# Gated mix of two memory attentions on one core: order of the short scores, the entry of P times v, the last output block, and a new table of rules

## The chip, the core and the metric

The kernel runs on one core of a Trainium2 chip. The time is device microseconds of one execution, the median of several runs. TensorE (PE) multiplies matrices out of SBUF into PSUM banks, VectorE (DVE), ScalarE (ACT) and GpSimd (POOL) do the elementwise work, and SyncE (SP) issues the DMAs.

## The reference

The input x has 2048 tokens of 640 features. Two attentions, A and B, with 32 heads of 20 features, are computed on it and mixed with a gate for each token. Each attention goes through four segments of 512 tokens. In a segment a query sees the keys of its own segment up to itself (a causal softmax), and a memory that sums up all earlier segments:

```python
logits = jnp.einsum("bhqd,bhkd->bhqk", qs, ks) * scale + mask
p = _softmax(logits, axis=-1)
a_dot = jnp.einsum("bhqk,bhkd->bhqd", p, vs)
num = jnp.einsum("bhld,bhde->bhle", phi(qs), M)      # M, z: sums over earlier segments
den = jnp.einsum("bhld,bhd->bhl", phi(qs), z)[..., None] + 1e-6
o = g * num / den + (1.0 - g) * a_dot                # g: one number for each head
M = M + jnp.einsum("bhld,bhle->bhde", phi(ks), vs)
z = z + jnp.einsum("bhld->bhd", phi(ks))
```

`phi(t)` is t + 1 above zero and exp(t) below. The o of all heads is multiplied by wo (640 x 640), and the result is gate * A + (1 - gate) * B.

## The kernel before

The work is cut into eight parts t = 0 to 7 (segment t // 2, attention t % 2), and each part's scores into eight *quads* of four heads, 64 quads in all. Every matrix of a product is split into two parts (high and low) that are multiplied in three combinations, (high, high), (low, high), (high, low).

**Two lanes.** Most matmuls use 64 or fewer of the 128 rows of TensorE's array. The kernel gives the lower half and the upper half of the rows a stream of matmuls each, the two *lanes*, and the two run side by side. P times v (`pv_unit`, L1396) uses all 128 rows, so it begins only when both lanes have ended, and the lanes begin again behind it. The update of the memory (L1029) may follow it directly.

**Units.** For each quad there are five S units (`s_unit`, L1283: query rows times keys, from which VectorE takes each query's maximum, L1268), five T units (`t_unit`, L1375: the scores again, transposed and with the maximum in two extra rows; ScalarE takes the exponential, L1367, and GpSimd cuts the triangle, L1368; the result is P) and one P times v. The causal triangle makes scores of 128, 256, 384 and 512 columns. `S_UNITS` and `T_UNITS` say which scores share a PSUM bank, and in which order their matmuls run: an entry (pair, block, offset) has 128 x (block + 1) columns in S units and 512 - 128 x block columns in T units. So of the S units the second and fourth have a 128 and a 384, and of the T units the third and fourth a 384 and a 128.

Between the units stand the *products* (`product`, recorded at L818): q, k and v of the next part, and the outputs. There are also transposes (`turn`, L971), in groups of four for each lane, and the reading of the memory (`mem_unit`, L929).

**The planner.** The order of the instructions is not written out. At build time a planner goes along with a modelled clock: `lane` holds when each lane ends, `lane_step` picks what a lane does next, and modelled events (DMAs landing, engines ending) set what can be picked. Where a lane has just ended on a matmul that is shorter than the loading of weights, `quick` is set for it, and `lane_step` then takes a waiting transpose first if there is one.

A table, `RULES`, has one line for each quad step i. Its fields: the order of the five S (of quad i + 2) and five T units (of quad i), and then `span`, `calm`, `lag`, `room`, `hold`, `wait`, `wait2` and `pair`. `wait` is how long a transpose waits for a quick lane before it is started as other work is. With `pair` 1 the P times v of quad i - 1 is held until the one after it can run too, and the two go back to back; a hold is not set where the P times v before it is held already.

`step` is the planner's loop. When a P times v is due and its P is there, it asks `aligned`: P times v goes if the two lanes end within 0.07 us of each other in the model, or after eight tries; each try that fails lets a lane take one more step.

**The end.** The last part's output is begun early for the first three of five row blocks of wo (`job_early`) and finished by `job_last` (L1210), with all 128 rows: for each of the five blocks of 128 output features three matmuls of 512 columns per remaining row block, and then `finish`: VectorE adds what was kept (L1195), and SyncE stores the block (L1197).

Of the kernel before, what the change touches and what calls it, by code (L numbers as in the profile page):

```python
# [18 lines left out]
P = 128  # L19
D = 640  # L20
# [22 lines left out]
def tile_gated_mix_infini_attn(  # L43
# [1142 lines left out]
    def job_last(t):  # L1186

        s = t // 2
        pps = {}

        def finish(m):
            if m not in kept:
                at(clk[0] + 0.3, lambda: finish(m))
                return
# [678 lines left out]
```

## Time and profile before

| | |
|---|---|
| median of 3 runs | 980.11 us (977.87 to 980.46) |
| profiled execution, its own time | 980.22 us |
| its span, first to last instruction | 978.4 us |
| TensorE busy | 968.8 us, 99% |
| VectorE, ScalarE, GpSimd busy | 75%, 69%, 64% |
| TensorE's granted clock, mean | 0.999 |
| DMA moved | 236.47 MB, 242 GB/s |

How to read it: an engine's busy time is the union of its instructions' spans, and a matmul's span covers its wait inside the array, so a TensorE that is 99% busy can still lose time between two matmuls. A group's row has its line, engine, operation, what it writes and reads, the shape, the count, and behind the first bar the busy time and the mean duration of one in ns; behind the second bar is the idle time before it. A row in order of time has its start, the time from its first start to its last end, and what ran; matmuls of both lanes stand in one list. A row of the waits has who waited, on whom, the sum in us, the count and the longest.

### The profile page before, as it was taken

The page shows a single profiled execution, that of the slowest core. Times are in us where ns is not written, and L with a number is a line of the kernel's source. Part 1 is how long each engine was busy: PE and PEld are TensorE (multiplying, and loading weights), DVE is VectorE, ACT ScalarE, POOL GpSimd, SP SyncE. Part 2 cuts the span into 40 slices and gives each one's busy share as a digit, 9 for nine tenths or more (in the row PEclk, how much of TensorE's full clock was granted, in tenths as well). Part 3 has the DMA queues.
Part 4 walks back from the last instruction along what each step waited for, and adds up shares of the span by engine and source line. Part 5 has one row for each costly group of instructions (what it writes and reads, how often), then busy time and mean ns, then how long its engine had stood idle before and what let it go on. Part 6 is the DMA issues. An engine that isn't in the chain of part 4 may idle for free.

```text
span 978.4 us, 31660 instructions
## 1 busy us (share of the span) xinstructions
PE 968.8 (99%) x11559; PEld 830.3 (85%) x11559; DVE 736.8 (75%) x2635; ACT 671.8 (69%) x1425; POOL 628.5 (64%) x1168
## 2 busy tenths in 40 slices
PE   9999999999999999999999999999999999999998
PEld 7998888888898888899878888798888888889785
DVE  4686777975787686886689986588676996788863
ACT  5476777777767587767676676676677666785672
POOL 4366657876568565768566577477765666666671
PEclk9999999999999999999999999999999999999999
DMA  6999988898888887977689777699777879877531
GB/s 214 309 312 260 298 259 286 252 301 269 257 282 243 268 269 218 305 216 228 190 244 294 225 222 208 206 296 289 216 231 235 271 223 264 242 227 240 155 92 54
DMA packets 146454, 236.47 MB, mean 242 GB/s; under 512 B 12950, under 2 KB 45883, under 8 KB 145979
## 3 DMA queue, kind: packets, MB, share of 16 engines
q1 hardware_dynamic: 146298, 234.46, 78.6%
q8 instruction: 91, 1.49, 0.7%
q14 instruction: 65, 0.52, 0.2%
HBM read 145.26 MB, written 94.65 MB: 245 GB/s over the span
## 4 chain that ended last, share of the span: by engine, by line
PE 91%; DMA 4%; DVE 1%; POOL 1%; issue 1%; ACT 1%; SPq 0%; ACTq 0%; POOLq 0%
PE bank L818 54%; PE bank L1396 14%; PE bank L1283 9%; PE bank L1375 7%; PE bank L929 3%; PE bank L971 3%; DMA wst<-in_a_wk_dram 1%; PE bank L1029 1%; DMA qst<-qd 1%; DMA kd<-row 1%; DMA kst<-kd 1%; PE bank L1210 0%; DVE row L1195 0%; POOL row L1502 0%; POOL row L1509 0%
## 5 line engine op out<-in xcount | busy, mean ns | idle before, releaser
L818 PE MATMUL bank<-row,wh 64*128 64x512 f32 x2308 | 484.9, 399 | 0.2
L818 PEld LDWEIGHTS bank<-row,wh 64*128 64x128 f32 x2308 | 319.8, 185 | 13.9 <-issue 1.6
L1268 DVE CUSTOM_DVE_ANT_0 junk<-bank,tri 128x128 bf16<-128x128 f32 (+2 forms) x768 | 278.9, 419 | 64.5 <-PE bank L1283 47.0
L1367 ACT ACTIVATE p<-bank 128x512 f32<-128x512 f32 x470 | 255.1, 601 | 89.7 <-PE bank L1375 75.5
L818 PE MATMUL bank<-row,wl 64*128 64x512 f32 x1154 | 297.4, 395 | 0.0
L1368 POOL TENSOR_SCALAR_AFFINE_SELECT p<-p 128x256 f32<-128x256 f32 (+1 forms) x470 | 171.9, 379 | 122.7 <-ACT p L1367 113.7
L555 POOL TENSOR_TENSOR wl<-wst,wh 128x640 fp32r<-128x640 f32 x115 | 179.8, 1569 | 68.6 <-ACT wh L557 62.8
L1268 DVE CUSTOM_DVE_ANT_0 bank<-bank,tri 128x512 f32<-128x512 f32 x256 | 172.5, 711 | 42.8 <-PE bank L1283 38.1
L1283 PE MATMUL bank<-kst,qst 60*128 60x128 f32 (+3 forms) x1024 | 179.5, 328 | 2.3 <-ACT p L1367 1.7
L818 PEld LDWEIGHTS bank<-row,wl 64*128 64x128 f32 x1154 | 176.7, 186 | 5.5 <-issue 0.6
L1375 PE MATMUL bank<-qst,kst 62*128 62x384 f32 (+3 forms) x1024 | 171.2, 316 | 0.0
L818 PE MATMUL bank<-wvh,row 64*128 64x320 f32 (+1 forms) x1280 | 169.7, 311 | 0.0
L818 PEld LDWEIGHTS bank<-wvh,row 64*128 64x128 f32 x1280 | 145.2, 186 | 2.2 <-issue 1.0
L1283 PEld LDWEIGHTS bank<-kst,qst 60*128 60x128 f32 x1024 | 129.6, 185 | 11.7 <-ACT p L1367 2.1
L1375 PEld LDWEIGHTS bank<-qst,kst 62*128 62x128 f32 x1024 | 129.0, 186 | 7.6 <-issue 1.0
L1396 PE MATMUL bank<-p,vst 128*32 128x128 f32 (+3 forms) x1536 | 117.5, 429 | 0.3 <-DVE mx L1268 0.3
L557 ACT CAST wh<-wst 128x640 fp32r<-128x640 f32 x119 | 86.9, 738 | 40.7 <-PE bank L818 18.1
L1367 ACT ACTIVATE row<-bank 128x512 f32<-128x512 f32 x170 | 92.8, 599 | 25.7 <-PE bank L1375 24.6
L1396 PEld LDWEIGHTS bank<-p,vst 128*32 128x32 f32 x1536 | 47.0, 110 | 67.5 <-issue 50.7
L1268 DVE DVE_READ_ACCUMULATOR2_ANT mx<- 128x1 f32 x1024 | 100.2, 98 | 0.0
L818 PE MATMUL bank<-wvl,row 64*128 64x320 f32 (+1 forms) x640 | 98.2, 310 | 0.0
L1368 POOL TENSOR_SCALAR_AFFINE_SELECT row<-row 128x128 f32<-128x128 f32 (+1 forms) x170 | 58.6, 352 | 54.9 <-ACT row L1367 50.4
(122 smaller groups left out, 1261.0 us busy)
## 6 DMA issues: line engine op xcount, KB each, us to landing
qst<-qd SPq DMA_DIRECT2D x128, 240.0 KB
kst<-kd SPq DMA_DIRECT2D x128, 240.0 KB
qd<-row SPq DMA_DIRECT2D x40, 512.0 KB
kd<-row SPq DMA_DIRECT2D x40, 512.0 KB
dots<-row SPq DMA_DIRECT2D x56, 256.0 KB
wst<-wmix SPq DMA_DIRECT2D x35, 320.0 KB
row<-dots SPq DMA_DIRECT2D x42, 256.0 KB
qd<-row SPq DMA_DIRECT2D x40, 256.0 KB
```

The source lines that it names most:

```text
L555: put(lo_eng, lo_cost, lambda: lo.tensor_tensor(out=wl, in0=w3, in1=r32(wh), op=ALU.subtract), end, prio=3)
L557: put("A", 0.625, lambda: nc.scalar.copy(wh, w3), low, prio=6)
L818: return nc.tensor.matmul(bank_of, lhsT=w[ROWS[half]], rhs=x_[ROWS[half]], start=start, stop=stop)
L929: return nc.tensor.matmul(pm[:, a - h0:c - h0, :].rearrange("p h e -> p (h e)"), lhsT=r32(pqTs[t, m][ROWS[half], P * n:P * (n + 1)]), rhs= ...
L971: return nc.tensor.transpose(px[:, n, r], block(n)[r], ident[r, r])
L1029: nc.tensor.matmul(v[r, a - LO[m]:c - LO[m], :].rearrange("p h e -> p (h e)"), lhsT=r32(pkn[:, P * n + r.start:P * n + r.stop]), rhs=vst[t ...
L1268: nc.vector.tensor_tensor_reduce(out=sc[:, off:off + w] if w == L else junk[:, at_:at_ + w], in0=sc[:, off:off + w], in1=tri[:, L - w:], s ...
L1283: lane_ops[half].append((mm(w), lambda pair=pair, qb=qb, off=off, w=w, r=r, sc=sc: nc.tensor.matmul(sc[:, off:off + w], lhsT=q[r, pair, P ...
L1367: put("A", 0.483, lambda: nc.scalar.activation(pt, sc, AF.Exp, scale=SCALE), lambda: (bank.give(sc), put("G", 0.15 + 0.105 * len(todo), la ...
L1368: "G", 0.15 + 0.105 * len(todo), lambda: nc.gpsimd.affine_select(out=blocks, in_=blocks, pattern=[[0, len(todo)], [1, P]], base=0, channel ...
L1375: lane_ops[half].append((mm(w), lambda pair=pair, kb=kb, off=off, w=w, r=r, sc=sc: nc.tensor.matmul(sc[:, off:off + w], lhsT=k[r, pair, P ...
L1396: nc.tensor.matmul(po[32 * j:32 * j + 32, P * kb:], lhsT=vst[t % 2][:, kb, h * E1:h * E1 + 32], rhs=pts[i, n, f][0][:, off:off + w], start ...
```

## The change

Four things. In `S_UNITS` the 384 now comes first and the 128 last. In `aligned`, where the last field of the table is 2 or 3, P times v waits until both lanes are quick, for up to 20 tries; the test of the last field for holding pairs becomes "odd". In `job_last` the three matmuls of the last block of the last row block are done twice with 256 columns, and `finish`, with its add and its DMA, once for each half. And all 66 lines of the table are new; six of them keep their order of units. Of the table the diff shows the lines with a last field other than 0, and the first.

```diff
--- before.py
+++ after.py
@@ -88,72 +88,72 @@
 
 
     RULES = {
-        0: "TSTSTSTSTS 1.06 2.38 0.22 8 2.7 1.07 1 0",
...
-        2: "TTSTTSSTSS 0.988 2.38 0.34 8 0 1.36 1 1",
...
-        4: "TSTSTSTSTS 1.01 2.38 0.3 8 0 1.6 1 1",
...
-        6: "SSTSTSTSTT 0.959 2.38 0.24 8 0 1.6 1 1",
...
-        15: "TTSSTTSSTS 1.01 2.38 0.26 8 0 1.6 1 1",
...
-        20: "STTSTSSTST 1.01 2.38 0.33 8 0.3 1.97 1 1",
...
-        23: "STTSTSSTST 1.01 2.38 0.4 0 0 1.6 0.84 1",
...
-        28: "TSTTSSTSTS 0.996 2.38 0.36 0 0 1.6 1.33 1",
-        29: "TSSTTSSTTS 1.01 2.38 0.3 8 0 1.6 1.69 1",
-        30: "TSTTSSTSTS 1.062 2.38 0.26 8 0 1.6 1.68 1",
...
-        38: "STSTSTSTST 1.01 3.5 0.23 2 0 1.85 0.41 1",
...
-        45: "TSTTSSTSTS 1.01 3.34 0.34 0 0 1.6 1 1",
...
-        47: "SSTSTSTSTT 0.903 2.4 0.26 8 0 1.6 1 1",
...
-        52: "STSTSTSTST 1.003 3.78 0.29 0 2.7 1.6 1.64 1",
-        53: "STSTSTSTST 1.01 2.38 0.3 8 0 1.6 1 1",
...
+        0: "TTSTTSSTSS 1.01 2.38 0.3 8 0 0.28 1.68 0",
...
+        2: "SSTSTSTSTT 0.992 3.2 0.3 2 0 0.82 0.39 3",
+        3: "STSTSTSTST 1.069 2.38 0.23 8 0 1.6 1.58 3",
...
+        5: "TSTTSSTSTS 1.01 2.38 0.3 8 1.9 1.6 1 1",
+        6: "STTSTSSTST 1.01 2.63 0.22 8 0 1.6 1 2",
+        7: "TSSTTSSTTS 0.995 2.03 0.31 10 0 1.6 1 2",
+        8: "TTSTTSSTSS 1.065 2.38 0.3 8 0 1.6 1 2",
...
+        17: "TSTSTSTSTS 1.01 2.38 0.3 0 0 1.6 1 2",
...
+        21: "STSTSTSTST 1.01 2.38 0.3 2 0 1.6 1 1",
...
+        23: "TTSSTTSSTS 1.01 2.38 0.34 8 0 1.6 0.49 3",
...
+        25: "TTTSSTSTSS 1.01 2.38 0.23 4 0 1.6 1 2",
...
+        28: "TTSSTTSSTS 0.95 2.86 0.38 2 1 1.6 0.81 2",
+        29: "TSTSTSTSTS 0.961 2.38 0.3 0 0.8 1.6 1 1",
...
+        35: "TSTSTSTSTS 1.015 4.08 0.23 8 0 1.6 1 2",
+        36: "TSTSTSTSTS 1.035 2.77 0.25 8 0 1.6 1.95 2",
+        37: "TTSTSTSTSS 1.013 1.44 0.4 8 0 1.6 1 3",
...
+        39: "TSTTSSTSTS 1 3.7 0.38 8 0 1.6 1 1",
...
+        41: "TSTSTSTSTS 1.01 2.38 0.3 8 0 0.2 1 2",
...
+        46: "STSTTSTSTS 1.037 2.81 0.36 10 0 1.6 1 1",
+        47: "TSTSTSTSTS 1.01 2.38 0.27 8 0 1.6 1 2",
...
+        49: "STTSTSSTST 1.01 3.19 0.3 0 0 1.12 1 3",
...
+        53: "TSTSTSTSTS 0.962 4.02 0.3 2 2.8 1.36 1.96 1",
...
+        60: "TSTSTSTSTS 1.01 2.38 0.4 6 0 2.11 0.67 2",
+        61: "TSTSTSTSTS 1.01 2.38 0.36 2 0 1.6 1 2",
...
     }
     rule = {}
     DONE = {"A": 0.27, "D": 0.26, "G": 0.22, "S": 0.0}
@@ -1188,14 +1188,15 @@
         s = t // 2
         pps = {}
 
-        def finish(m):
+        def finish(m, a=0, w=L):
             if m not in kept:
-                at(clk[0] + 0.3, lambda: finish(m))
+                at(clk[0] + 0.3, lambda: finish(m, a, w))
                 return
-            put("D", 0.605, lambda: nc.vector.tensor_tensor(
-                out=r32(kept[m]), in0=pps[m], in1=r32(kept[m]), op=ALU.add), lambda: dma(
-                    0.7, lambda: nc.sync.dma_start(
-                        out=outT[P * m:P * (m + 1), L * s:L * (s + 1)], in_=r32(kept[m])), prio=2), prio=2)
+            part = r32(kept[m])[:, a:a + w]
+            put("D", 0.08 + w / 975.0, lambda: nc.vector.tensor_tensor(
+                out=part, in0=pps[m][:, a:a + w], in1=part, op=ALU.add), lambda: dma(
+                    0.7 * w / L, lambda: nc.sync.dma_start(
+                        out=outT[P * m:P * (m + 1), L * s + a:L * s + a + w], in_=part), prio=2), prio=2)
 
         for k in range(SOON, KT):
             yield from hold_on(lambda: (t, k) in OTs, "last")
@@ -1205,13 +1206,17 @@
                 if m not in pps:
                     yield from hold_on(lambda: bank.free, "bank")
                     pps[m] = bank.free.pop(0)
-                for j, (w, o) in enumerate(((wh, oh), (wl, oh), (wh, ol))):
-                    yield from hold_on(lambda: not any((*firsts, *seconds, *lane_ops)), "last")
-                    whole(STEP, lambda: nc.tensor.matmul(
-                        pps[m], lhsT=w[:, k, :], rhs=o, start=(k == SOON and j == 0), stop=(k == KT - 1 and j == 2)))
-                    yield STEP
-                if k == KT - 1:
-                    after_whole(lambda m=m: finish(m))
+                ends = k == KT - 1 and m == KT - 1
+                for a in (0, L // 2)[:1 + ends]:
+                    c = L // 2 if ends else L
+                    for j, (w, o) in enumerate(((wh, oh), (wl, oh), (wh, ol))):
+                        yield from hold_on(lambda: not any((*firsts, *seconds, *lane_ops)), "last")
+                        whole(0.122 if ends else STEP, lambda: nc.tensor.matmul(
+                            pps[m][:, a:a + c], lhsT=w[:, k, :], rhs=o[:, a:a + c],
+                            start=(k == SOON and j == 0), stop=(k == KT - 1 and j == 2), skip_group_check=m == KT - 1))
+                        yield STEP
+                    if k == KT - 1:
+                        after_whole(lambda m=m, a=a, c=c: finish(m, a, c))
 
 
     def quad(i):
@@ -1244,7 +1249,7 @@
     t_done, p_done, s_left = {}, {}, {}
 
 
-    S_UNITS = (((0, 3, 0),), ((0, 0, 384), (0, 2, 0)), ((0, 1, 0), (1, 1, 256)), ((1, 0, 384), (1, 2, 0)), ((1, 3, 0),))
+    S_UNITS = (((0, 3, 0),), ((0, 2, 0), (0, 0, 384)), ((0, 1, 0), (1, 1, 256)), ((1, 2, 0), (1, 0, 384)), ((1, 3, 0),))
 
     T_UNITS = (((0, 0, 0),), ((1, 0, 0),), ((0, 1, 0), (0, 3, 384)), ((1, 1, 0), (1, 3, 384)), ((0, 2, 0), (1, 2, 256)))
 
@@ -1716,6 +1721,8 @@
         tries[0] += 1
         if abs(max(lane[0], now[0]) - max(lane[1], now[0])) > 0.07 and tries[0] < 8:
             return False
+        if rule["pair"] > 1 and tries[0] < 20 and not all(quick):
+            return False
         tries[0] = 0
         return True
 
@@ -1798,7 +1805,7 @@
                     s_unit(j, n)
         if 1 <= i < 65:
             pv_due.append(i - 1)
-            if rule["pair"] and i < 64 and i - 2 not in pv_held:
+            if rule["pair"] % 2 and i < 64 and i - 2 not in pv_held:
                 pv_held.add(i - 1)
         todo = list(rule["order"])
         at_ = {"S": 0, "T": 0}
```

93 rows, old and new, of the table RULES are left out of this document.

## The prediction

> **What bounds the kernel now.** I read the page first, then the groups of TensorE with shapes kept apart, the waits of TensorE, and TensorE's order of time around a few units. The page says which engine it is:
>
> ```profile
> span 978.4 us, 31660 instructions
> PE 968.8 (99%) x11559; PEld 830.3 (85%) x11559; DVE 736.8 (75%) x2635; ACT 671.8 (69%) x1425; POOL 628.5 (64%) x1168
> PE 91%; DMA 4%; DVE 1%; POOL 1%; issue 1%; ACT 1%; SPq 0%; ACTq 0%; POOLq 0%
> PE bank L818 54%; PE bank L1396 14%; PE bank L1283 9%; PE bank L1375 7%; PE bank L929 3%; PE bank L971 3%; DMA wst<-in_a_wk_dram 1%; PE bank L1029 1%; DMA qst<-qd 1%; DMA kd<-row 1%; DMA kst<-kd 1%; PE bank L1210 0%; DVE row L1195 0%; POOL row L1502 0%; POOL row L1509 0%
> ```
>
> TensorE is busy all the time, and the chain that ends last is 91% its own work. The other engines have a quarter of their time free, so no edit on them counts except in the last microseconds. The matmuls' work is the same before and after. What can change is (1) how the two lanes (lower and upper half of the array) lose time between matmuls, (2) the few true stalls, and (3) the end.
>
> True stalls are small. The waits of TensorE, whole kernel:
>
> ```profile
> PE bank L1283 <- ACT p L1367: 1.7, 1, 1.7
> PE bank L356 <- DVE qst L360: 1.5, 1, 1.5
> PE bank L1283 <- DMA kst<-kd: 0.6, 1, 0.6
> PE bank L929 <- ACT mr L714: 0.5, 1, 0.5
> PE bank L1396 <- DVE mx L1268: 0.3, 1, 0.3
> ```
>
> Without the warm-up's 1.5 us they come to 1.7 + 0.6 + 0.5 + 0.3 = 3.1 us. So the losses that matter hide inside "busy", and one of them is what the change aims at: the 128-column matmul. The order of time shows it:
>
> ```profile
> 97.08 0.46 PE L1283 MATMUL bank<-kst,qst 60*128 60x128 f32 x4
> 97.37 0.63 PE L818 MATMUL bank<-row,wh 64*128 64x512 f32 x3
> ...
> 133.25 0.34 PE L1375 MATMUL bank<-qst,kst 62*128 62x384 f32 x1
> ...
> 133.43 0.22 PE L1375 MATMUL bank<-qst,kst 62*128 62x128 f32 x1
> 133.49 0.22 PE L971 MATMUL bank<-ident,row 64*128 64x64 f32 x1
> ```
>
> In a P unit (L1375) the 384 starts at 133.25 and the 128 at 133.43: the long one takes 0.18. The transpose behind the 128 starts 0.06 later, so the short one takes 0.06. Together 0.24. In an S unit (L1283, "x4" is a 128 and a 384 in each lane) the next matmul starts at 97.37, 0.29 after the short one. So **a short score costs its lane about 0.05 us** beyond its columns: I read it as the weights of a later matmul not being there in time. The groups by shape say the same for all 256 of them:
>
> ```profile
> L1283 PE MATMUL bank<-kst,qst 60*128 60x384 f32 x256 | 66.4, 388 | 0.0
> L1375 PE MATMUL bank<-qst,kst 62*128 62x384 f32 x256 | 62.6, 347 | 0.0
> ```
>
> A 384 behind the short one (S, L1283) lasts 388 ns, a 384 ahead of it (P, L1375) 347: 41 ns. I take 0.05. Over 256 S shorts in two lanes that is 256 x 0.05 / 2 = 6.4 us, the most that the new order could ever return.
>
> **The change part by part.** *Short one last in S units.* Nothing is added or taken away: same matmuls, same two VectorE maxima per bank, read in the other order. The 0.05 does not vanish; it moves to whatever follows the unit. If a long matmul follows, the balance is zero. It is saved if a transpose follows, for the transpose at 133.49 shows no delay; the planner looks for one whenever a lane has just ended on a short matmul. There are not many:
>
> ```profile
> L971 PE MATMUL bank<-ident,row 64*128 64x64 f32 x304 | 32.5, 226 | 0.2
> L971 PE MATMUL bank<-ident,O 64*128 64x64 f32 x240 | 18.2, 228 | 0.1
> ```
>
> 544 transposes, four to a lane's turn, are 136 starts; P units' shorts already offer as many places as S units now will. Bounds: 0 and 136 x 0.05 / 2 = 3.4 us saved. A transpose waits only 1.6 us for such a place by the table, so I take about a quarter: **-0.8 us**.
>
> *P times v waits for two short ends.* 17 of the 66 lines have 2 or 3 in the last column (lines 2, 3, 6, 7, 8, 17, 23, 25, 28, 35, 36, 37, 41, 47, 49, 60, 61). It adds no instruction; up to 20 steps of the planner's loop pass before P times v (L1396) goes anyway. Entry today, and what a block takes:
>
> ```profile
> 382.11 0.39 PE L818 MATMUL bank<-row,wl 64*128 64x512 f32 x1
> 382.43 2.36 PE L1396 MATMUL bank<-p,vst 128*32 128x512 f32 x32
> ...
> 973.14 0.40 PE L1210 MATMUL bank<-row,wvh 128*128 128x512 f32 x1
> 973.38 0.40 PE L1210 MATMUL bank<-row,wvl 128*128 128x512 f32 x1
> 973.61 0.39 PE L1210 MATMUL bank<-row,wvh 128*128 128x512 f32 x1
> ```
>
> A 512-column step is 0.235 (973.38 to 973.61), and from the last 512 to P times v 0.32 pass: 0.09 of entry, paid whatever came before. Behind a short end this 0.09 stands in place of the 0.05, so each waiting entry saves up to 0.05 in both lanes: 17 x 0.05 = 0.85, or nothing where the 20 steps run out. I take **-0.6**. Two lanes that end on the same unit's short also tend to end level. Today they need not:
>
> ```profile
> 304.07 0.39 PE L818 MATMUL bank<-row,wh 64*128 64x512 f32 x1
> 304.10 0.60 PE L818 MATMUL bank<-row,wl 64*128 64x512 f32 x2
> 304.62 0.62 PE L1396 MATMUL bank<-p,vst 128*32 128x512 f32 x2
> ```
>
> Three 512s lie in 304.07 to 304.70; the last ends 0.39 after 304.31, and the one that runs in the other lane started at 304.10, 0.2 earlier, so one lane idles 0.2 longer than the other. If half of 17 entries win 0.1 of one lane, that is 17 x 0.5 x 0.1 / 2 = **-0.4** (bounds 0 and 17 x 0.2 / 2 = 1.7). What waits behind the held P times v: its P rows, its bank, the evacuation and, at the end, the transposes. Other matmuls of the two lanes run meanwhile, and that is the cover; without it, see the slower rival.
>
> *Fewer pairs.* Two P times v back to back (odd last column) share an entry:
>
> ```profile
> 382.50 4.45 PE bank L1396 x64
> 396.34 2.29 PE bank L1396 x32
> ```
>
> Two single ones cost 2 x 2.29 + 0.09 = 4.67 against 4.45: 0.22. Of the odd lines 14 become 11; a line whose pair would overlap the last one falls out (29 and 53 before, 3 after), so 12 become 10: **+0.4** (bounds 0 and 3 x 0.22 = 0.7).
>
> *The last block in halves.* The end of the kernel:
>
> ```profile
> 974.04 0.69 DVE L1195 TENSOR_TENSOR row<-bank,row 128x512 f32<-128x512 f32 x1
> 974.76 0.33 SPq L1197 DMA_DIRECT2D out_dram<-row  x1
> ...
> L1549 DVE TENSOR_TENSOR row<-bank,fw 128x320 f32<-128x320 f32 x8 | 3.9, 491 | 0.3
> ```
>
> VectorE's adds stand back to back, so the first half can't start before 974.04 though its three matmuls are through sooner. A half: 512 columns take 0.69, 320 take 0.49, thus 256 about 0.42; two are 0.85, 0.16 later than now. SyncE issues two DMAs instead of one; the first (0.33) fits into the second half's add, so the last issue is 0.16 later too. The last transfer then has half the bytes. The five transfers fill the queues from the tenth to the 28th slice of 0.2 us:
>
> ```profile
> DMA  0000000009996998999899999964000000000000
> ```
>
> 19 x 0.2 / 5 = 0.76 each, so the shorter one saves 0 (if the fixed part is all) to 0.38. Net +0.16 to -0.22; I take **-0.1**, nearer the full saving since the queues are full to the end.
>
> *The table.* 60 of 66 orders change, so nearly all work moves to other moments. The matmuls do not change, hence only the stalls and the lane losses do. The largest stall belongs to one place:
>
> ```profile
> 602.46 0.56 PE L1283 MATMUL bank<-kst,qst 60*128 60x128 f32 x4 [1.67 <-ACT p L1367]
> ...
> 596.26 4.54 DMA qst<-qd
> ```
>
> It hangs on a transfer (the chain runs 4.54 us through it) that the planner held to be earlier. Another order will not repeat it there, but has its own. Bounds: all 3.1 us gone, or as much again added; I take half of the large one, **-0.9**.
>
> Sum: -0.8 - 0.6 - 0.4 + 0.4 - 0.1 - 0.9 = -2.4 us. The profiled execution took 980.22 us, 1.8 more than its span, and the median of the runs is 980.11 (977.87 to 980.46), so the execution is a usual one. **977.7 us**, 0.25% less. A measurement of this kernel tells about 0.3%, 2.9 us, from no change: faster is below 977.2, slower above 983.0.
>
> **The rivals.** *Much faster:* the plan finds a use for most short ends. Half of the 6.4 us (3.2), the waiting entries in full (0.85), the stalls (3.1), less 0.4 for the pairs and 0.1 at the end: 980.1 - 6.9 = 973.3. For it: the 41 ns stand behind every S short. Against it: only 136 transposes and 17 entries are there to take them.
>
> *Slower:* the held P times v keeps its P rows, so the next unit's P has no room, ScalarE has no exponentials to do, and when the fill work runs dry TensorE stands. 20 steps are ten in each lane, 10 x 0.235 = 2.3 us of delay. One such stop is priced by the 1.67 of line 1283. Three of 17 waits that end so cost 5.0, and the lost pairs 0.4: 985.5. It decides from three stops on, as the saved 2 us then are gone too. For it: the P rows are ten fixed ones and the rest comes from a shared store. Against it: ScalarE is 69% busy and the products, over half of the chain, need no P.
>
> *The change does not do what it says:* behind two short ends the entry grows. The nearest row is P times v behind transposes in both lanes:
>
> ```profile
> 941.96 0.40 PE L971 MATMUL bank<-ident,O 64*128 64x64 f32 x4
> 942.29 0.62 PE L1396 MATMUL bank<-row,vst 128*32 128x512 f32 x2
> ```
>
> The four end 942.36; a transpose lasts 0.22, so the last began at 942.14 and 0.15 pass to the entry, of which it streams some 0.06: 0.09 to 0.12. Then the entries give 0 to 0.85 less, transposes find no more places than now, and the table's stalls come back in other places: 0.4 - 0.1 = 980.4. The Trainium skill, "TensorEngine Tiling (Array Packing)", section "Key Properties", speaks for this rival: it says that changing the tiling mode drains the engine. By that rule an entry from two lanes into 128-row matmuls is a drain, whose length need not shrink with the last matmul; the 0.15 behind a transpose against 0.32 behind a 512 says that most of it does.
>
> **How the numbers follow.** Forecast 0.42 (975.5 to 980 by itself), much faster 0.23, slower 0.16, no effect 0.19. Of the forecast's share some 0.17 lies below 977.2. Faster: 0.23 + 0.17 = 0.40; slower: 0.16 + 0.01 = 0.17; the rest, 0.43, within. The range goes from 971.5 (the faster rival and a little) to 983.5, short of the slower one: 0.05 left out below, 0.14 above.
>
> **What would show it.** Right: the 384 of L1283 falls from 388 to about 347 ns; L1396 pieces of x64 in the chain are fewer by about two; L1195 shows six adds, two of 256; TensorE's waits sum to less than 3 us. The slower rival: new waits of TensorE on ScalarE's p above 1 us. The faster one: the products of 512 columns (L818) get shorter than their 399 and 395 ns:
>
> ```profile
> L818 PE MATMUL bank<-row,wh 64*128 64x512 f32 x2308 | 484.9, 399 | 0.2
> L818 PE MATMUL bank<-row,wl 64*128 64x512 f32 x1154 | 297.4, 395 | 0.0
> ```
>
> The prediction is wrong if the stalls, not the short ends, carry the difference by more than 3 us in either direction.

## The result, and the profile after

The change made the kernel slower: 986.26 us (983.58 to 994.70, nine executions) against 980.11 (977.87 to 982.59, nine); the ratio is 1.0070, 95% interval 1.0050 to 1.0091. The forecast of 977.7 us and its range up to 983.5 were wrong, and so was the sign. In all, 21 executions of the changed kernel have a median of 986.8 us. The one that is profiled here, 994.70 us, is the slowest of them, so the main readings are taken again from two others, in experiments 1 and 3. One execution of the kernel before, run beside the experiments, took 2381 us; it is left out of every number.

The page of the changed kernel, profiled execution, shows the same picture as before, with a chain that is 86% TensorE in place of 91% and 6% DMA in place of 4%:

```profile
span 992.8 us, 31649 instructions
...
PEclk9999999899999999999999899999999999999999
...
PE 86%; DMA 6%; POOL 2%; DVE 2%; ACT 1%; issue 1%; SPq 1%; DVEq 0%; ACTq 0%; POOLq 0%
```

The line of the clock is new: it falls in the eighth and the 23rd slice. Before the change it stayed full up to the last slice.

The waits of TensorE in the same execution:

```profile
PE bank L1288 <- ACT p L1372: 2.1, 2, 1.1
PE bank L929 <- ACT p L1372: 1.8, 1, 1.8
```

Three stops for `p` (the exponentials of ScalarE) come to 3.9 us, where before there was one of 1.7. L1288, L1380, L1372 and L1401 are the lines 1283, 1375, 1367 and 1396 of before.

TensorE's groups, shapes apart:

```profile
L1288 PE MATMUL bank<-kst,qst 60*128 60x384 f32 x256 | 59.7, 345 | 0.0
L818 PE MATMUL bank<-row,wh 64*128 64x512 f32 x2308 | 490.6, 404 | 0.2
L818 PE MATMUL bank<-row,wl 64*128 64x512 f32 x1154 | 296.5, 401 | 0.0
```

The 384 of the S units fell from 388 to 345 ns, as the prediction said. The products of 512 columns rose from 399 and 395 to 404 and 401 ns; a part of that is half clock in this execution (below), for in experiment 3 the first are at 402.

VectorE's groups from 960 us to the end show the halves:

```profile
L1196 DVE TENSOR_TENSOR row<-bank,row 128x512 f32<-128x512 f32 x4 | 2.8, 692 | 1.2 <-PE bank L1214 1.2
L1196 DVE TENSOR_TENSOR row<-bank,row 128x256 f32<-128x256 f32 x2 | 0.8, 420 | 0.0
```

**What ends behind the three stops.** ScalarE in order of time, in the changed kernel, at the three places (the bracket is the idle time before the row, and who ended it):

```profile
180.26 0.72 ACT L557 CAST wh<-wst 128x640 fp32r<-128x640 f32 x1 [2.37 <-DMA wst<-in_a_wq_dram]
551.46 0.62 ACT L1504 CAST row<-row 128x512 fp32r<-128x512 f32 x1 [2.21 <-DMA dots<-row]
892.95 0.60 ACT L777 ACTIVATE row<-bank 128x512 f32<-128x512 f32 x1 [2.10 <-DMA kd<-row]
893.45 0.59 ACT L1372 ACTIVATE p<-bank 128x512 f32<-128x512 f32 x1
```

And TensorE behind them:

```profile
183.06 0.50 PE L1288 MATMUL bank<-kst,qst 60*128 60x512 f32 x1 [0.97 <-ACT p L1372]
552.62 0.34 PE L929 MATMUL bank<-mbd,row 64*128 64x84 f32 x1 [1.78 <-ACT p L1372]
894.09 0.50 PE L1288 MATMUL bank<-kst,qst 60*128 60x256 f32 x3 [1.09 <-ACT p L1372]
```

At each place ScalarE has reached an instruction for which a transfer must land. It lands 2.1 to 2.4 us after ScalarE was free. An exponential is queued behind it, starts 0.5 us after it without a wait of its own (893.45 behind 892.95), and so comes late, and TensorE stands 1.0 to 1.8 us.

**The clock.** The granted clock by stretches, changed kernel (us of the span, length, busy times, then PEclk, DMA share and GB/s):

```profile
178.00:184.80 6.80, 5.83 (x39) 4.53 (x36) 3.98 (x7) 4.54 (x9) 6.48 (x9) 1.00 1.00 283
184.80:191.60 6.80, 6.74 (x28) 5.15 (x28) 4.89 (x10) 5.02 (x11) 5.46 (x6) 0.50 0.82 298
553.40:560.20 6.80, 6.80 (x49) 6.52 (x48) 3.33 (x10) 1.89 (x4) 2.27 (x4) 0.50 0.49 166
956.20:959.60 3.40, 3.40 (x21) 1.43 (x24) 2.23 (x8) 3.19 (x9) 3.40 (x9) 0.50 0.01 2
```

For 6.8 us behind the stop at 183, for 6.8 behind the one at 552, and for 3.4 at 956, TensorE ran at half its clock. Of work that fills TensorE this costs half the stretch: (6.8 + 6.8 + 3.4) / 2 = 8.5 us in this execution.

### The profile page after: what moved, and what is told of

Same layout as the page of the kernel before. It is cut to its first block, busy times and chain, and to the rows that moved or that the text cites. A ratio compares the mean times of both kernels' runs of the same rounds, so it can differ in the third digit from the quotient of the medians.

```text
span 992.8 us, 31649 instructions
## 1 busy us (share of the span) xinstructions
PE 980.6 (99%) x11562; PEld 833.1 (84%) x11562; DVE 742.0 (75%) x2638; ACT 674.5 (68%) x1426; POOL 625.3 (63%) x1165
## 4 chain that ended last, share of the span: by engine, by line
PE 86%; DMA 6%; POOL 2%; DVE 2%; ACT 1%; issue 1%; SPq 1%; DVEq 0%; ACTq 0%; POOLq 0%
PE bank L818 51%; PE bank L1401 13%; PE bank L1288 7%; PE bank L1380 7%; PE bank L929 3%; PE bank L971 2%; DMA kst<-kd 1%; DMA dots<-row 1%; PE bank L1029 1%; PE bank L868 1%; DMA qd<-row 1%; DMA kd<-row 1%; DMA beta<-in_b_beta_dram 1%; DMA row<-dots 1%; ACT p L1372 1%
## 5 line engine op out<-in xcount | busy, mean ns | idle before, releaser
L818 PE MATMUL bank<-row,wh 64*128 64x512 f32 x2308 | 490.6, 404 | 0.2
L1372 ACT ACTIVATE p<-bank 128x512 f32<-128x512 f32 x492 | 268.8, 601 | 91.5 <-PE bank L1380 72.8
L1273 DVE CUSTOM_DVE_ANT_0 junk<-bank,tri 128x384 bf16<-128x384 f32 (+2 forms) x768 | 283.5, 420 | 54.3 <-PE bank L1288 31.5
L1373 POOL TENSOR_SCALAR_AFFINE_SELECT p<-p 128x256 f32<-128x256 f32 (+1 forms) x492 | 179.7, 378 | 150.9 <-ACT p L1372 141.3
L1380 PE MATMUL bank<-qst,kst 62*128 62x384 f32 (+3 forms) x1024 | 177.5, 318 | 0.4 <-ACT p L1372 0.2
L1288 PE MATMUL bank<-kst,qst 60*128 60x384 f32 (+3 forms) x1024 | 173.9, 315 | 3.3 <-ACT p L1372 2.1
L1288 PEld LDWEIGHTS bank<-kst,qst 60*128 60x128 f32 x1024 | 131.3, 185 | 11.9 <-ACT p L1372 2.7
L1380 PEld LDWEIGHTS bank<-qst,kst 62*128 62x128 f32 x1024 | 133.4, 187 | 8.5 <-issue 1.6
L1401 PE MATMUL bank<-p,vst 128*32 128x256 f32 (+3 forms) x1612 | 124.3, 432 | 0.0
L1401 PEld LDWEIGHTS bank<-p,vst 128*32 128x32 f32 x1612 | 49.8, 110 | 71.5 <-issue 52.1
L1372 ACT ACTIVATE row<-bank 128x512 f32<-128x512 f32 x148 | 81.0, 597 | 21.9 <-PE bank L1380 19.3
L818 PEld LDWEIGHTS bank<-wvl,row 64*128 64x128 f32 x640 | 82.4, 186 | 0.5 <-issue 0.2
```

The source lines that it names most:

```text
L818: return nc.tensor.matmul(bank_of, lhsT=w[ROWS[half]], rhs=x_[ROWS[half]], start=start, stop=stop)
L1273: nc.vector.tensor_tensor_reduce(out=sc[:, off:off + w] if w == L else junk[:, at_:at_ + w], in0=sc[:, off:off + w], in1=tri[:, L - w:], s ...
L1288: lane_ops[half].append((mm(w), lambda pair=pair, qb=qb, off=off, w=w, r=r, sc=sc: nc.tensor.matmul(sc[:, off:off + w], lhsT=q[r, pair, P ...
L1372: put("A", 0.483, lambda: nc.scalar.activation(pt, sc, AF.Exp, scale=SCALE), lambda: (bank.give(sc), put("G", 0.15 + 0.105 * len(todo), la ...
L1373: "G", 0.15 + 0.105 * len(todo), lambda: nc.gpsimd.affine_select(out=blocks, in_=blocks, pattern=[[0, len(todo)], [1, P]], base=0, channel ...
L1380: lane_ops[half].append((mm(w), lambda pair=pair, kb=kb, off=off, w=w, r=r, sc=sc: nc.tensor.matmul(sc[:, off:off + w], lhsT=k[r, pair, P ...
```

## The experiments

**1. The change once more.**

> The changed kernel once more, to see what its profile shows in another execution. Theory (stalls): the two stops of TensorE near 183 and 552 us come from this plan and stand in the same places, 1 to 2 us each; the 6.8 us at half clock behind them need not come again each time, so the profiled time is between 983 and 995. Rival (the plan's own lanes): no stop above 0.5 us, and still 985.

Measured: 987.74 us, ratio 1.0079 (1.0064 to 1.0094). The span of the profiled execution is 987.6, 5.2 less than above, with the same places. ScalarE in order of time:

```profile
180.14 0.73 ACT L557 CAST wh<-wst 128x640 fp32r<-128x640 f32 x1 [1.53 <-DMA wst<-in_a_wq_dram]
548.97 0.62 ACT L1504 CAST row<-row 128x512 fp32r<-128x512 f32 x1 [1.56 <-DMA dots<-row]
887.80 0.60 ACT L777 ACTIVATE row<-bank 128x512 f32<-128x512 f32 x1 [2.54 <-DMA kd<-row]
```

The clock by stretches, same execution, shows half clock twice, for 3.4 us, at the first place and near 952:

```profile
186.20:189.60 3.40, 3.40 (x17) 3.31 (x19) 2.81 (x5) 2.81 (x6) 3.40 (x4) 0.51 0.92 354
950.70:954.10 3.40, 3.40 (x26) 1.83 (x28) 2.62 (x10) 3.13 (x8) 3.38 (x9) 0.51 0.01 2
```

ScalarE's waits belong to the plan: they return at the same instructions. TensorE's stops behind them are 0.12, 1.12 and 1.53 us this time. What differs is how long they are and how much half clock follows; at the first place it follows a stop of TensorE of only 0.12 us.

**2. The new order of S, in the plan of before.**

```diff
+    def last_short(todo):
+        return todo[::-1] if len(todo) > 1 and todo[0][1] == 0 else todo
...
-            for j, (pair, qb, off) in enumerate(todo):
+            for j, (pair, qb, off) in enumerate(last_short(todo)):
                 w = P * (qb + 1)
+                planned = P * (todo[j][1] + 1)
```

The maxima are read in the new order too; the planner still charges the old order, so every other instruction stays where it was.

> The kernel before with every instruction where it was, only the 128 and the 384 of an S unit exchanged in their lanes. Theory (the 0.05 us only moves to the next matmul): no change, within 1 us of the kernel before. Rival (the short one last is worth something, or costs something, by itself): 2 to 6 us off, either way. The 384 of the S units falls from 388 to about 347 ns in both cases; where the cost moves, the products' mean rises by some ns.

Measured: 981.21 us, ratio 1.0025 (1.0011 to 1.0038). TensorE's groups:

```profile
L1287 PE MATMUL bank<-kst,qst 60*128 60x384 f32 x256 | 61.6, 347 | 0.3 <-ACT mr L714 0.3
L818 PE MATMUL bank<-row,wh 64*128 64x512 f32 x2308 | 487.5, 401 | 0.2 <-DVE mx L1271 0.2
L818 PE MATMUL bank<-row,wl 64*128 64x512 f32 x1154 | 298.1, 398 | 0.0
```

The 384 gains 41 ns, 256 x 41 = 10.5 us summed over both lanes. The products lose 2 and 3 ns: 2308 x 2 + 1154 x 3 = 8.1 us. The 0.05 us behind a short score left the 384 and arrived at the products. The mean over all of them hides at which. One such place, TensorE in order of time:

```profile
157.55 0.22 PE L1287 MATMUL bank<-kst,qst 60*128 60x128 f32 x1
157.61 0.44 PE L818 MATMUL bank<-row,wl 64*128 64x512 f32 x1
...
157.89 0.39 PE L818 MATMUL bank<-row,wh 64*128 64x512 f32 x1
```

The product right behind the short score lasts 0.44 us, and the next one of its lane starts 0.28 after it instead of 0.23. The profile doesn't name a matmul's lane, but the order in which the kernel issues them does: the 173 products of 512 columns right behind a short S score last 443 ns, the 2445 behind another such product 392. So the delay is at the matmul right behind.

In this plan the order returns nothing; it costs 1.3 us by the medians (981.21 against 979.8), 1 to 4 by the ratio. That lies between the theory (within 1 us) and the rival (2 or more).

**3. The old order of S, in the plan of after.** The same edit the other way round, and the changed kernel beside it.

```diff
+    def short_first(todo):
+        return todo[::-1] if len(todo) > 1 and todo[-1][1] == 0 else todo
...
-            for j, (pair, qb, off) in enumerate(todo):
+            for j, (pair, qb, off) in enumerate(short_first(todo)):
                 w = P * (qb + 1)
+                planned = P * (todo[j][1] + 1)
```

> The kernel after, every instruction where its plan has it, except that in the second and fourth S unit of each quad the 128 runs ahead of the 384 again, as in the kernel before (the planner still charges the 384 first). The 384 of S should last 388 ns again in place of 345, and the products of 512 columns 2 to 3 ns less. The same edit the other way round, in the plan of the kernel before, cost 1.3 us. Theory A (the order costs about 1.3 us in any plan, since the 0.05 only moves to another matmul and adds some): 1.3 us less than the kernel after run beside it. Theory B (the plan of after was made for the short last, and uses 21 places behind it for transposes where before used 11): 0 to 2 us more. In both the stops behind late transfers near 183, 550 and 889 us stay.

> The kernel after unchanged, to stand beside the one with the 128 first: 986 to 988 us, with the stops near 183, 550 and 889 us.

Measured: 988.55 us with the 128 first, 988.22 for the changed kernel beside it; ratios to before 1.0077 (1.0056 to 1.0098) and 1.0075 (1.0052 to 1.0098). Groups with the 128 first, and then of the changed kernel:

```profile
L818 PE MATMUL bank<-row,wh 64*128 64x512 f32 x2308 | 484.9, 400 | 0.2
L1292 PE MATMUL bank<-kst,qst 60*128 60x384 f32 x256 | 64.9, 387 | 0.0
```

```profile
L818 PE MATMUL bank<-row,wh 64*128 64x512 f32 x2308 | 488.1, 402 | 0.2
L1288 PE MATMUL bank<-kst,qst 60*128 60x384 f32 x256 | 59.1, 345 | 0.2 <-ACT mr L714 0.2
```

The exchange is the same: 42 ns off the 384, 2 ns on the products. In this plan the order makes no difference that can be measured. The 0.3 us are known to some 3 us only, so theory A, 1.3 us less, is not excluded. What is shown is that the order doesn't make the loss: with the old one it is still there, 5.5 us or more. With the 128 first the stops at 547 and 889 stayed (1.36 and 1.15 us); the one near 183 was under 0.15, other than expected.

This third execution of the changed kernel holds a warning. TensorE's two waits for `p` are

```profile
PE bank L1288 <- ACT p L1372: 1.1, 2, 0.8
PE bank L929 <- ACT p L1372: 0.5, 1, 0.5
```

1.6 us, as much as the one stop of before, and yet the span is 986.6. The sum of the stops doesn't measure what the late transfers cost. One reason stands in TensorE's order of time at the first place:

```profile
182.66 0.50 PE L1288 MATMUL bank<-kst,qst 60*128 60x512 f32 x1 [0.24 <-ACT p L1372]
183.00 1.31 PE L818 MATMUL bank<-row,wl 64*128 64x512 f32 x5
184.16 2.40 PE L818 MATMUL bank<-row,wh 64*128 64x512 f32 x7
```

Five products take 183.00 to 184.16, 0.23 each: that is the pace of one lane. By the kernel's order the other lane's last matmul starts at 181.35 and its next at 185.77. Of these 4.4 us it works for 0.23; the rest costs half its length, and no view counts it as idle time. The clock shows another part; two stretches of 20 us are not at 1.00:

```profile
180.00:200.00 20.00, 19.70 (x195) 15.41 (x193) 15.94 (x44) 17.26 (x33) 16.02 (x20) 0.91 0.97 314
...
940.00:960.00 20.00, 19.77 (x207) 12.35 (x207) 12.38 (x48) 14.81 (x34) 14.49 (x33) 0.91 0.25 83
```

**4. The halves alone.** The kernel before with the new `finish` and `job_last` of the diff.

> The kernel before with only the last block in halves; all else stands where it was. Theory: from 0.2 us longer to 0.2 us shorter, no change that can be measured. Rival (the halved stores cost a second fixed part): 1 to 2 us longer between the last add and the end.

Measured: 979.85 us, ratio 1.0002 (0.9990 to 1.0015). Nothing, as expected.

**5. Stops of known length.** Ten times, at the entry of P times v, TensorE is made to wait for copies of VectorE, in the kernel before:

```diff
+    STALLS = {6: 1, 12: 2, 18: 3, 24: 4, 30: 1, 36: 2, 42: 3, 48: 4, 54: 2, 60: 1}
...
+            nc.tensor.matmul(po, lhsT=tri[:, :P], rhs=tri, start=True, stop=True)
+            for _ in range(STALLS[i]):
+                nc.vector.tensor_copy(junk, po)
+            nc.tensor.matmul(po, lhsT=junk[:, :P], rhs=junk, start=True, stop=True)
```

> The kernel before, with ten stops of TensorE put in ahead of ten P times v: it waits for one to four copies of a bank by VectorE (0.7 us each), started by a matmul of its own. Extra work, nothing left out. Theory (a stop takes the clock down): some stops above 1 us are followed by about 7 us at half clock, which cost 3 to 4 us more than the stop itself; 23 copies are 16 us, so 1000 us or more. Rival (the half clock has another cause): the clock stays full, the time is the sum of the stops, 996 to 1000 us.

Measured: 1009.03 us, ratio 1.0297 (1.0279 to 1.0315), 29 us more. TensorE's idle times at the ten stops are 1.11 to 3.28 us, 20.5 in sum, more than the 16 us of copies. One row in order of time, and the clock by stretches behind it:

```profile
406.77 4.06 PE L1406 MATMUL bank<-p,vst 128*32 128x512 f32 x32 [3.28 <-DVE junk L1389]
...
407.00:410.40 3.40, 3.40 (x24) 1.08 (x20) 1.55 (x6) 1.25 (x3) 2.01 (x3) 0.50 1.03 249
```

Of the ten this is the only stop behind which half clock followed in the profiled execution (span 1003.3, 24.9 above before); another as long, at 787, had none. Of the 24.9 us the stops are 20.5, half clock 3.4 / 2 = 1.7, and 2.7 are left for the twenty matmuls put in. This execution is the fastest of the four; the others, 1008.55 to 1011.21 us, have a mean clock of 0.992 to 0.995 in place of 0.998, so more half clock. The theory's 1000 us or more is met, but mainly because the stops were longer than foreseen. So a stop costs its length, and now and then half clock besides; its length alone doesn't decide that.

**6. Fewer bytes, before and after.** Transfers that land sooner, with the plan of each kernel unchanged:

```diff
+    def part_of(i):
+        return 2 if i > 16 else KT
...
+                c = VN // 4 if i > 16 else VN
+                dma(0.53 * n, lambda: nc.sync.dma_start(out=w3[:, :, :c], in_=src[m // 4][:, a:b, :c]), landed, prio=need[i], lat=2.6)
...
+                    dma(0.95, lambda dst=dst, src=rows[half], half=half, n=L // 2 if i >= NQ else L: nc.sync.dma_start(
```

> The kernel before, every instruction where it was, but from the fifth quad on a quad's load brings half of its columns, and from the 18th job on a weight load brings two of five blocks (of wv a quarter of the columns); the rest of the tiles keeps old values. So 50 MB of 236 are left out. Theory (TensorE's stops come from transfers that land later than planned): the lag behind the planner's own clock stays near 2 to 2.5 us all along (3.7 at the end before), the stop at 602 is gone, 978 to 979.5 us. Rival (the order itself): no change, 980.

> The changed kernel with the same bytes left out. The planner's own clock ends at 973.8 us for it, at 972.0 for the kernel before, 1.8 us later. Theory (late transfers make the rest): the stops at 183, 550 and 889 us shrink or go, no half clock, 980 to 982 us, some 2 us above the kernel before with fewer bytes and 5 below the changed kernel. Rival (the short ends and the waits of P times v cost by themselves): 985 or more, as with all bytes.

Measured: before 978.81 us, ratio 0.9982 (0.9968 to 0.9996); after 983.42, ratio 1.0033 (1.0018 to 1.0047), both to the kernel before on the same chip. By the traces 58.7 of 236.5 MB were left out, not 50. In the kernel before the stop at 602 is gone, but another of 1.2 us came near 469. With the plan of after, the longest wait of TensorE behind the warm-up is this:

```profile
PE bank L1294 <- DVE row L1586: 0.6, 1, 0.6
```

The three stops for `p` are gone, and ScalarE's waits for the transfers behind two of them tell why. Changed kernel first, fewer bytes second:

```profile
ACT row L777 <- DMA kd<-row: 5.8, 2, 3.7
ACT row L1504 <- DMA dots<-row: 2.2, 1, 2.2
```

```profile
ACT row L782 <- DMA kd<-row: 0.7, 1, 0.7
```

So the late transfers make those stops. But most of the distance to before stays, 983.42 - 978.81 = 4.6 of some 6.7 us: more than the theory allowed, less than the rival asked.

At the first place the stop is gone, and one lane still stands. TensorE in order of time, and two stretches of 3.4 us:

```profile
182.08 1.33 PE L823 MATMUL bank<-row,wl 64*128 64x512 f32 x5
...
180.80:184.20 3.40, 3.40 (x18) 2.67 (x17) 3.09 (x4) 3.40 (x8) 3.33 (x6) 1.00 0.48 105
184.20:187.60 3.40, 3.34 (x29) 2.61 (x29) 1.87 (x3) 3.32 (x7) 3.40 (x4) 1.00 1.02 393
```

TensorE is busy for all of the first stretch, with 18 matmuls in place of 29. One lane's last matmul starts at 180.92 and its next at 184.86, 3.9 us, of which it works 0.23; ScalarE waits for no transfer there. This stand is in the plan: in the planner's own clock this lane stands 1.4 us near 179 and 3.1 us near 181, because no product can begin (first the next weights are not split yet, then no bank is free). The plan of before has no such stand over 1.03 us.

**7. Code without its table, table without its code.** The new order of S and the halves with the table of before; and the new table in the code of before, with 2 read as 0 and 3 as 1. A P times v that is held for a pair is let go when the planner has nothing left to do; without that neither mix can be planned to its end.

```diff
-        if pv_due and pv_due[0] in pv_held and len(pv_due) > 1:
+        if pv_due and pv_due[0] in pv_held and (len(pv_due) > 1 or not events and not any(seconds)):
```

> The changed code with the table of before (and a held P times v let go where the planner would otherwise have nothing left to do). Theory (a table fits one code alone, and the planner's clock tells): the planner's clock ends at 1100.5 us, so about 1104 to 1115 us. Rival (the code's parts are worth 2 us and the table little): 975 to 990.

> The code of before with the new table (its last field only odd or even; a held P times v let go as in the other). Theory (a table fits one code alone): the planner's clock ends at 1116.3 us, so 1120 to 1135. Rival (the new table alone makes the 6 us): 984 to 988.

Measured: 1105.91 and 1111.65 us, 13% slower, one execution each. The planner's own clock, which ends at 972.0 us for before and 973.8 for after, ends at 1100.5 and 1116.3 for these: it came within 0.5%, 5.4 us too low and 4.7 too high. A part of that is luck: the mean granted clock is 0.967 and 0.958 in these two, so up to 36 and 47 us are half clock, which the planner doesn't model. The clock tells a plan that is 13% longer; a difference of 1.8 us it can't vouch for. Each table goes with its own code. So the parts of the diff can't be valued one by one against the table. What can be compared is what each plan was to take. By its own clock, **the plan of after is 1.8 us longer than that of before**.

The second of these kernels holds a P times v behind two short scores, at full clock. TensorE in order of time:

```profile
992.92 0.41 PE L1375 MATMUL bank<-qst,kst 62*128 62x384 f32 x4
993.26 0.62 PE L1396 MATMUL bank<-p,vst 128*32 128x512 f32 x2
```

Four matmuls, a 384 and a 128 in each lane. From the start of the last 128 to P times v pass 0.148 us, of which the 128 streams 0.06: 0.09 of entry, without the 0.05.

**8. One line of the table each.** Line 37 of before (with the halves), and three late lines of after, both with the letting go of experiment 7:

```diff
-        37: "TSSTTSSTTS 0.917 2.38 0.26 0 0 1.6 0.36 0",
+        37: "STTSTSSTST 0.917 2.38 0.26 0 0 1.6 0.36 0",
...
-        53: "TSTSTSTSTS 0.962 4.02 0.3 2 2.8 1.36 1.96 1",
+        53: "TTSTSTSTSS 0.962 4.02 0.3 2 2.8 1.36 1.96 1",
-        55: "STSTSTSTST 1.01 2.38 0.3 8 0 1.6 0.25 0",
+        55: "STSTSTSTST 1.01 3.32 0.3 8 0 1.6 0.25 0",
-        59: "TSTSTSTSTS 1.01 2.61 0.3 8 0 2.54 0.36 0",
+        59: "TSTSTSTSTS 1.01 2.61 0.3 8 0 1.37 0.36 0",
```

> The kernel before with the last block in halves (which by itself changed nothing measurable) and one entry of its table changed: line 37's order becomes STTSTSSTST. The matmuls are the same. The planner's own clock ends at 972.2 as with the halves alone, but the work between 580 and 620 us lies elsewhere, so the exponential that came late at 602 us (stop of 1.67) should not. Theory (stops behind late transfers are what a table carries beside its own clock): the stop at 602 goes or another comes in its place; without one the run is 978 to 979, 1 to 2 us below the kernel before. Rival (the time hangs on how the lanes use short ends, not on stops): 979.9, no change.

> The kernel after with three late entries of its table changed: line 53's order TTSTSTSTSS, line 55's fourth number 3.32 in place of 2.38, line 59's wait for a transpose 1.37 in place of 2.54. The planner's own clock ends at 974.0, 0.2 above the kernel after. Theory (stops behind late transfers and half clock behind thin stretches make up what the planner's clock does not show): the stops before 860 us stay (183, 551), the one at 889 and the thin stretch near 945 are drawn anew and may go: 984 to 987, at most 3 us less than the kernel after. Rival (the new order of S units, the wait and the plan's own length make all of the loss, wherever the stops are): 986 to 988, no change.

Measured: 979.83 us for line 37, beside 981.04 of before, ratio 0.9992 (0.9978 to 1.0006): not told from no change. The stop near 602 stayed, at 1.11 us instead of 1.67. With the late lines 985.93, ratio 1.0055 (1.0034 to 1.0076). TensorE at the third place:

```profile
888.47 0.50 PE L1288 MATMUL bank<-kst,qst 60*128 60x256 f32 x3 [0.50 <-ACT p L1372]
...
948.00:954.00 6.00, 5.74 (x60) 3.32 (x61) 5.13 (x18) 5.96 (x15) 6.00 (x15) 1.00 0.10 36
```

The stop is 0.50 us there, and the stretch near 950 runs at full clock in this execution. Half clock came once before the end, for 3.4 us at 187. The time lies 0.3 to 2.3 us under the medians of the three series of after, within their intervals. The trace fits the theory; the times alone can't tell it from the rival.

## Why the prediction was wrong

The loss of some 6 to 8 us has four parts. Two of them can be sized by sorting the executions by their mean granted clock: where it was 0.999 or more, no stretch of half clock is taken to stand before the end (each of 3.4 us takes 0.5 x 3.4 / 980 = 0.0017 off the mean, and no profiled execution with such a clock has one).

| mean us of executions | clock 0.999 or more | all |
|---|---|---|
| before (71 executions beside the experiments) | 979.9 (63 of them) | 980.2 |
| after (21) | 985.4 (8) | 987.2 |
| before, fewer bytes (10) | 978.7 (10) | 978.7 |
| after, fewer bytes (10) | 982.0 (4) | 983.2 |

- **Half clock**: 987.2 - 985.4 = 1.8 us, for which before has 980.2 - 979.9 = 0.3: 1.5 more. In 12 of 21 executions of after the clock was under 0.998; these average 988.6. With fewer bytes 983.2 - 982.0 = 1.2 us of it stay in after, so the three stops are not its only cause.
- **Late transfers**: without half clock after is 985.4 - 979.9 = 5.5 above before, with fewer bytes 982.0 - 978.7 = 3.3. So 2.2 us hang on when transfers land. They come from 8 and 4 executions, and are known to about 1.4 us.
- **The plan itself**: 1.8 us, by the planner's own clock. No run isolates this, and experiment 7 doesn't show the clock to be good to 2 us. But one place can be seen in every trace of this plan: the lane that stands near 181 (experiment 6), 3.7 / 2 = 1.9 us even with fewer bytes.
- **The rest**: 5.5 - 2.2 - 1.8 = 1.5 us. No run assigns it, and it is as large as the uncertainty of the others.

Now the steps as the prediction put them.

*The table, -0.9, was the step that failed.* It said that the matmuls do not change, "hence only the stalls and the lane losses do", and then priced only the stalls, by half of one stop, as if the old plan's worst place were more telling than 60 unseen orders. The mechanism that it named, an order that puts work ahead of a transfer which lands late, is right: it came back in three places. Two things were put at nothing without a reason. The new plan can lose more lane time, and did: 1.8 us by its own clock, 1.9 us seen at one place. And half clock may follow a stop or a standing lane: 1.5 us more than before. The bound of 3.1 us more was too small for that: with the two it had to reach about 6. The last sentence of the prediction, that it is wrong if the stalls carry more than 3 us, is borne out in part: late transfers and half clock together are 2.2 + 1.5 = 3.7 us, but not all of the half clock belongs to stalls.

*The order of S, -0.8.* Measured: nothing that can be told in the plan of after, +1.3 in that of before. The 41 ns were read rightly (388 to 345), and so was "it moves to whatever follows". The step that failed is the quarter of 136 places for transposes. In the plan of after 17 of 256 short scores of S are followed by a transpose (L971) in their lane, 11 before; those of T fell from 15 to 11. Two more places are 2 x 0.05 / 2 = 0.05 us. (The 21 in the expectation of experiment 3 is 17 when each lane's order is followed.)

*P times v behind two short ends, -0.6 and -0.4.* No run isolates it, and the traces show no gain. In the plan of after 13 of 54 entries from two lanes come under the wait. Twelve run out of their 20 tries, like this one, where both lanes end on products, TensorE in order of time:

```profile
464.99 1.32 PE L818 MATMUL bank<-row,wh 64*128 64x512 f32 x8
466.24 0.64 PE L1401 MATMUL bank<-p,vst 128*32 128x512 f32 x4
```

In the planner's clock the lanes of these twelve end 0.11 us apart, those of the other 42 entries 0.04: the wait went with less level ends, where the -0.4 counted on more level ones. The thirteenth, at 948.89, finds both lanes quick, one behind a short S score and one behind a transpose; the lane of the score has stood for 0.3 us by then. The prediction had this as a bound ("nothing where the 20 steps run out") and gave it too little weight: two lanes must both have just ended on one of the few short matmuls, at the same moment. The price itself was right: the entry behind two short scores in experiment 7 saves the 0.05, and so does one at 945.46 in the trace of after with fewer bytes, to which no wait applied (0.15 us from the start of the last short one). There the rule for which the Trainium skill was named, "TensorEngine Tiling (Array Packing)", section "Key Properties", that a change of the mode drains the engine, agrees with the 0.09 us that stay. One row was misread: ahead of the entry at 942.29 the four transposes are all of one lane, and the other ended on a 512 of S; the entry at 536.54 has transposes in both, and 0.15 us too.

*Fewer pairs, +0.4.* Blocks of 64 are 10 instead of 11, one less and not two: 0.2 us.

*The halves, -0.1.* Right within what can be measured: +0.0002 of the time, interval -0.0010 to +0.0015. The half add took 420 ns, as the 0.42 worked out from 512 and 320 columns.

*The slower rival, 985.5,* met the number and its sign in the trace (waits of TensorE for `p` of 1.0 to 1.8 us), but by another mechanism, so the number was luck. It had ScalarE without work, because a held P times v keeps its rows. At the three places ScalarE had work: it stood behind a transfer.

*Much faster* and *no effect* fell: the products got longer, not shorter, and the time moved.

## What to carry to other kernels

An engine whose queue runs in order passes a late transfer on to everything behind the waiting instruction: look at which transfers stand ahead of the work that feeds the bottleneck, not only at the transfers that the bottleneck itself waits for. A small local gain that needs a new schedule is worth less than the spread between schedules: here 0.05 us a short score against some 2 us for one lane that stands and up to 1.8 us for a transfer that lands late. With two lanes, look for stretches in which one of them stands: TensorE counts as busy there. And a delay that comes from the stream of a lane moves to the next matmul of that lane unless something that doesn't suffer from it is put there; compare the groups of all shapes before calling it saved.

## What the runs showed of the hardware

Half clock came in stretches of 3.4 us or whole multiples of it (6.8; up to 20.5 in the second kernel of experiment 7), and it needed no long stop. In the third execution of the changed kernel TensorE stops for 0.24 us at 182.4, and half clock begins at 185.8. By stretches of 3.4 us ahead of it:

```profile
178.60:182.00 3.40, 3.40 (x29) 2.83 (x26) 2.58 (x4) 2.13 (x4) 3.21 (x5) 1.00 1.03 257
182.00:185.40 3.40, 3.16 (x14) 2.14 (x12) 2.28 (x3) 3.40 (x8) 3.33 (x6) 1.00 1.01 351
```

The clock is still full and TensorE busy for 3.16 of 3.40 us, but with 14 matmuls instead of 29, since one lane stands (experiment 3). Six traces have this place. From the start of the standing lane's last matmul to its next 5.7 us pass in the first execution of the changed kernel, and 6.8 us of half clock follow. Where 4.3, 4.4 and 4.6 us pass (experiment 1, experiment 3, the late lines of experiment 8), 3.4 us follow; where 3.9 pass (the 128 first, and fewer bytes), none. So the length of the stand goes with it; TensorE's idle time there was 0.97, 0.12, 0.24, 0.85 us, and under 0.1 in the last two. No run varies one without the other. On the other side nine of the ten stops of 1.1 to 3.3 us that were put in had no half clock behind them in the profiled execution. The Trainium skill, "TensorE: Matmul & The Clock Gate", section "HAM oscillation — how this bites in real kernels", gives as its rule that there be no idle gaps of TensorE above about 3.4 us. These traces don't bear it out as the threshold: half clock followed much shorter gaps.

A short score's 0.05 us goes to the matmul right behind it in its lane: a 384 lasts 388 ns there in place of 347, a product of 512 columns 443 in place of 392 (experiment 2). A transpose doesn't show it: 222 ns behind a short S score in the first execution of the changed kernel, 224 behind another transpose. In a mean of all 3462 products it shows as 2 to 3 ns each and looks spread out.
